# The second pass of a batch set as one block behind chunk 1 of the next first pass, and gathered MoE rows used ten stages after their issue

## The chip, the cores and the metric

One core of a Trainium2 chip runs the whole program. The metric is the device time of one execution in microseconds; the median of three runs of the kernel before is 342.16 us (341.62 to 342.59).

## What is computed

Four batches of q, k and v, each 6208 x 256 in float32. Per batch a cross-covariance attention over the 256 channels, and then a mixture-of-depths MoE over its output: the 128 rows with the highest gate score get a small feed-forward added, all other rows pass through.

```python
qn = q / (np.linalg.norm(q, axis=1, keepdims=True) + 1e-06)   # norm over the 6208 rows
kn = k / (np.linalg.norm(k, axis=1, keepdims=True) + 1e-06)
s = kn.transpose(0, 2, 1) @ qn / tau                          # 256 x 256 a batch
a = softmax(s)                                                # over the last axis
x = v @ a
scores = x @ w_gate
top = the 128 rows of a batch with the highest score
out = x;  out[top] += sigmoid(scores[top]) * (relu(x[top] @ w1) @ w2)
```

## The kernel before

A batch is cut into six chunks of 1024 rows (each partition holds 8 rows of it) and a remainder of 64 rows, counted as chunk 6. Loads convert float32 to bf16 on the way.

**First pass** (`p1_steps`, L195): per row set of 128 rows six matmuls, into the 256 x 256 product of k and q (L210) and into the Gram blocks of q and k (L212, L214), from whose diagonal the norms come. All q and k of a batch have to be in before its softmax. **Softmax** (`softmax_stages`, L222): a generator with three stages; VectorE makes the norms (L229 to L256), a matmul with ones spreads them (L259), then exponentials on ScalarE and the matrix a, with its product with the gate weights, `aw_sb` (L284). **Second pass** (`p2_transpose` L299, `p2_out` L327): per group of four row sets eight transposes of v on TensorE, a copy to SBUF on VectorE (L309), then output matmuls (L343) and score matmuls (L322); ScalarE evicts the output (L348), and a chunk of 1 MB goes out on SyncE's queue (L353). **MoE** (`moe_stages`, L357): a generator that yields between its stages. Stage 1 takes the maximum of the scores, stages 2 to 8 are seven steps of a search for the threshold (VectorE compares and counts, L389, L393, and one small matmul sums over the partitions, L401), stages 9 to 11 make the list of the 128 row numbers `idx` (L427, L438, L453). Then an indirect DMA on POOL's queue gathers these rows of v (`vg`, L455), four yields later TensorE transposes them (L462), multiplies by a (L468), transposes again (L477), does the feed-forward (L495, L503), and a second indirect DMA scatters the updated rows over the output (L510), when the plain stores of that batch have been issued.

**Order.** `phase(b)` (L92) writes out by hand how the chunks of the first pass of batch b and the second pass of batch b-1 follow each other. The list rules two things: the loads (`units`) and, cut into halves of a chunk, TensorE's work (`atoms`). For batches 1 to 3 it is qk0 qk1 v0 v1 qk2 v2 v3 qk3 v4 v5 qk4 v6 qk5 qk6, where qk is of batch b and v of batch b-1. After every atom `slot()` (L526) advances the waiting softmax and the oldest waiting MoE by one stage each. Every engine runs its instructions in the order in which they are written, so a stage that waits on TensorE holds all matmuls behind it, and a gather or scatter that waits on POOL holds all loads behind it.

**Buffers.** q and k have five chunk buffers each, v has six, the outputs nine, the transposed v fourteen. `pump` (L132) issues loads in the order of `units` on POOL's queue as soon as, in the order of the program, the next chunk has a free buffer; it stops at the first that has none.

**The end.** For batch 3 the loop over v makes transposes and scores alone (L579 to L589, with a `slot()` of its own at L589 beside the one after each atom, so two stages a group). Chunks 2 to 6 of the output of batch 2 are held back until then (`deferred`). Then, group by group, one stage of the MoE of batch 3 and the output of one group of batch 3 alternate (L606 to L611), and the rest of that MoE follows.

Of the kernel before, what the change touches and what calls it, by code (L numbers as in the profile page):

```python
# [26 lines left out]
def kernel(  # L27
# [14 lines left out]
    B, N, C = q.shape  # L42
# [7 lines left out]
    NFULL = N // CHUNK  # L50
# [6 lines left out]
    V_BUFS = 6  # L57
    ST_BUFS = 9
    VT_BUFS = 14
    HOLD_FROM = 2  # L60

    const = ctx.enter_context(tc.tile_pool(name="const", bufs=1))
# [2 lines left out]
    rem_pool = ctx.enter_context(tc.tile_pool(name="rem_pool", bufs=2))  # L65
    vt_pool = ctx.enter_context(tc.tile_pool(name="vt_pool", bufs=VT_BUFS))
    st_pool = ctx.enter_context(tc.tile_pool(name="st_pool", bufs=ST_BUFS))
# [24 lines left out]
    def phase(b):  # L92
        if b == 0:
            return [("qk", 0, ci) for ci in range(NFULL + 1)]
        if b == B:
            return [("v", B - 1, ci) for ci in range(NFULL + 1)]
        items = []
        nv = 0
        for ci in range(NFULL + 1):
            items.append(("qk", b, ci))  # L100
            if ci >= 1:
                for _ in range(2 if ci < NFULL // 2 + 1 else NFULL + 1):
                    if nv <= NFULL:
                        items.append(("v", b - 1, nv))
                        nv += 1
        return items

    units = [u for b in range(B + 1) for u in phase(b)]
    loaded = {}
    load_inst = {}  # L110
# [21 lines left out]
    def pump(most=1000):  # L132
        while state["next"] < len(units) and most > 0:
            u = units[state["next"]]
            bk = bucket(u[0], u[2])
            if state[bk] >= limit[bk]:
                return
            emit_load(u)
            state[bk] += 1
            state["next"] += 1  # L140
            most -= 1

    def consumed(u):
        state[bucket(u[0], u[2])] -= 1
        pump()
# [49 lines left out]
    def p1_steps(b, ci):  # L195

        if b not in acc:
            acc[b] = (ps_s.tile([P, 2, C], F32, name="s_ps"), ps_g.tile([P, 4, P], F32, name="g_ps"))
        s_ps, g_ps = acc[b]
        qt, kt = loaded[("qk", b, ci)]  # L200
        rows = RPP if ci < NFULL else 1
        parts = P if ci < NFULL else REM

        def step(s):
            first = ci == 0 and s == 0
            last = ci == NFULL
            qs, ks = qt[:parts, s, :], kt[:parts, s, :]
            for cc in range(2):
                sl = slice(cc * P, (cc + 1) * P)
                nc.tensor.matmul(s_ps[:, cc, :], lhsT=ks[:, sl], rhs=qs,  # L210
                                 start=first and cc == 0, stop=last and cc == 1)
                nc.tensor.matmul(g_ps[:, cc, :], lhsT=qs[:, sl], rhs=qs[:, sl],  # L212
                                 start=first and cc == 0, stop=False)
                nc.tensor.matmul(g_ps[:, 2 + cc, :], lhsT=ks[:, sl], rhs=ks[:, sl],  # L214
                                 start=False, stop=last and cc == 1)

        return [lambda s=s: step(s) for s in range(rows)]
# [94 lines left out]
    def p2_score(b, g, vt_sb, js):  # L312
        ci, s0, n = g
        parts = P if ci < NFULL else REM
        aw_sb = a_tiles[b][1]
        if ci == 0 and s0 == 0 and js[0] == 0:
            sc_tiles[b] = ps_sc.tile([P, NCOL, 2], F32, name="sc_ps")
        sc_ps = sc_tiles[b]
        for j in js:
            col = ci * RPP + s0 + j  # L320
            for cc in range(2):
                nc.tensor.matmul(sc_ps[:parts, col, :], lhsT=vt_sb[:, cc, j, :parts],  # L322
                                 rhs=aw_sb[:, cc, :],
                                 start=cc == 0 and col in (0, NCOL - 1),
                                 stop=cc == 1 and col >= NCOL - 2)

    def p2_out(b, g, vt_sb, scores):  # L327
        ci, s0, n = g
        parts = P if ci < NFULL else REM
        a_sb = a_tiles[b][0]  # L330
        if s0 == 0:
            if ci < NFULL:
                stage_of[(b, ci)] = st_pool.tile([P, RPP, C], F32, name="stage")
            else:
                stage_of[(b, ci)] = rem_pool.tile([P, 1, C], F32, name="stage_rem")
        st = stage_of[(b, ci)]
        for pair in range((n + 1) // 2):
            o_ps = ps_o.tile([P, 2, C], F32, name="o_ps")
            m = min(2, n - pair * 2)
            for pj in range(m):  # L340
                j = pair * 2 + pj
                for cc in range(2):
                    nc.tensor.matmul(o_ps[:parts, pj, :], lhsT=vt_sb[:, cc, j, :parts],  # L343
                                     rhs=a_sb[:, cc, :], start=pj == 0 and cc == 0,
                                     stop=pj == m - 1 and cc == 1)
                if scores:
                    p2_score(b, g, vt_sb, [j])
            nc.scalar.copy(st[:parts, s0 + pair * 2:s0 + pair * 2 + m, :], o_ps[:parts, :m, :])  # L348

    def emit_store(b, ci):  # L350
        st = stage_of.pop((b, ci))
        if ci < NFULL:
            return nc.sync.dma_start(out=view(out, b, ci), in_=st)  # L353
        return nc.sync.dma_start(out=view(out, b, ci), in_=st[:REM, 0, :])


    def moe_stages(b):  # L357
# [29 lines left out]
        for i in range(NSTEP):  # L387
# [18 lines left out]
            if i + 1 < NSTEP:  # L406
# [44 lines left out]
                                op1=ALU.min)  # L451
        idx = moe.tile([P, 1], I32, name="idx", bufs=2)
        nc.vector.tensor_scalar(out=idx, in0=fl, scalar1=float(b * N), scalar2=None, op0=ALU.add)  # L453
        vg = moe.tile([P, C], BF16, name="vg")
        nc.gpsimd.indirect_dma_start(out=vg, out_offset=None, in_=v_flat,  # L455
                                     in_offset=bass.IndirectOffsetOnAxis(ap=idx[:, 0:1], axis=0))
        for _ in range(4):
            yield
        a_sb, _ = a_tiles[b]
        tp = ps_vt.tile([P, 2, 4, P], BF16, name="vt_ps")  # L460
# [41 lines left out]
        for fc in range(NFC):  # L502
# [2 lines left out]
        upd = moe.tile([P, D], F32, name="upd", bufs=2)  # L505
        nc.vector.scalar_tensor_tensor(out=upd, in0=y_ps[:, 0, :], scalar=gate, in1=xe, op0=ALU.mult,
                                       op1=ALU.add)
        while held[b] or (b >= B - 2 and deferred):
            yield
        nc.gpsimd.indirect_dma_start(out=out_flat[0:(b + 1) * N, :],  # L510
# [6 lines left out]
    def advance(lst):  # L517
        while lst:
            try:
                next(lst[0])  # L520
                return True
            except StopIteration:
                lst.pop(0)
        return False

    def slot():  # L526
        advance(smx_side)
        advance(side)
# [31 lines left out]
    def transposes(i, ahead):  # L560

        while tq and tpos[tq[0]] <= i + ahead:
            _, b, g = tq.pop(0)
            vts[(b, g)] = p2_transpose(b, g)
            if g[1] == 4 or g[0] == NFULL:
                consumed(("v", b, g[0]))

    last_groups = []
    for i, a in enumerate(atoms):
        if a[0] == "p1":  # L570
            _, b, ci, lo_, hi_ = a
            pump()
            st = p1_steps(b, ci)
            for f in st[lo_:hi_]:
                f()
            if hi_ != 4:
                consumed(("qk", b, ci))
        elif a[0] == "smx":
            smx_side.append(softmax_stages(a[1]))  # L579
            advance(smx_side)  # L580
        else:
            _, b, g = a
            if b == B - 1:
                transposes(i, 2)
                while b not in a_tiles:
                    advance(smx_side)
                p2_score(b, g, vts[(b, g)], list(range(g[2])))
                last_groups.append(g)
                slot()  # L589
            else:  # L590
                while b not in a_tiles:
                    advance(smx_side)
                p2_out(b, g, vts.pop((b, g)), True)
                if g[1] == 4 or g[0] == NFULL:
                    held[b] -= 1
                    if b == B - 2 and g[0] >= HOLD_FROM:
                        deferred.append((b, g[0]))
                    else:
                        emit_store(b, g[0])
                if g[0] == NFULL:  # L600
                    side.append(moe_stages(b))
        transposes(i, 2)
        slot()
    side.append(moe_stages(B - 1))
    flush_deferred()
    for g in last_groups:  # L606
# [42 lines left out]
```

## Time and profile before

| | us |
|---|---|
| median of three runs | 342.16 (341.62 to 342.59) |
| the profiled execution | 343.5 |
| its span, first to last instruction | 341.4 |
| TensorE matmuls busy | 216.0 (63%) |
| VectorE busy | 139.9 (41%) |
| ScalarE busy | 67.3 (20%) |
| POOL busy | 56.0 (16%) |
| mean granted TensorE clock | 0.807 of 2.4 GHz |

The span is the time between the first and the last instruction that the profiler saw; what lies around it, 2.1 us, belongs to the execution. Busy shares are means over stages with different limits: the first two thirds move nearly all loads, the rest is mostly computation. So the views by stretch and in order of time say more than the table. In them a number in brackets behind an instruction is the time that its engine stood idle before it, and what ended that.

### The profile page before, as it was taken

To read this page: it belongs to the slowest core of one execution; us is meant where nothing else is said; L and a number is where in the kernel's file an instruction comes from. 1 tells how busy PE (TensorE), PEld (TensorE's weight loads), DVE (VectorE), ACT (ScalarE), POOL (GpSimd) and SP (SyncE) were. 2 spreads that over 40 slices of the span, in tenths; PEclk is the share of its full clock that TensorE was granted. 3 is DMA by queue.
4 is the path that set the end of the run, shared out by engine and by line. 5 is a ranking of instruction groups with operands and counts; after the bars stand their busy time and mean duration, and the time that the engine had idled before them with its cause. 6 is when DMAs were issued, how large, how long until landed. Compare 5 with 4: busy or idle time off the path is not lost.

```text
span 341.4 us, 6038 instructions
## 1 busy us (share of the span) xinstructions
PE 216.0 (63%) x2524; PEld 186.0 (54%) x2524; DVE 139.9 (41%) x550; ACT 67.3 (20%) x133; POOL 56.0 (16%) x103
## 2 busy tenths in 40 slices
PE   0878259999575489205898089658981336957350
PEld 0767248999454278204798068647981225835230
DVE  0000044332017796101234889212349895588120
ACT  1000001534200105001450012214500100255410
POOL 7212322110121212030123002101100001100110
PEclk9999767999768599755999569969997555798855
DMA  7999999999999999999879999943594000046800
GB/s 126 213 214 207 213 213 214 213 310 312 323 265 217 213 213 228 316 213 213 294 144 290 245 214 181 293 121 63 99 374 172 0 1 10 17 183 262 307 0 15
DMA packets 17353, 65.90 MB, mean 193 GB/s; under 512 B 1968, under 2 KB 4656, under 8 KB 14256
## 3 DMA queue, kind: packets, MB, share of 16 engines
q0 software_dynamic: 13408, 39.98, 60.5%
q1 hardware_dynamic: 3920, 25.56, 18.6%
q8 instruction: 19, 0.31, 0.3%
q14 instruction: 6, 0.05, 0.0%
HBM read 79.04 MB, written 25.95 MB: 308 GB/s over the span
## 4 chain that ended last, share of the span: by engine, by line
DMA 37%; issue 26%; PE 18%; DVE 11%; POOL 3%; ACT 1%; POOLq 1%; SPq 0%; DVEq 0%; ACTq 0%
DMA k_ch<-in_k_dram 27%; DMA v_ch<-in_v_dram 5%; DMA vg<-in_v_dram,idx 4%; PE o_ps L343 4%; PE s_ps L210 4%; PE vt_ps L306 3%; DVE cnt L393 2%; PE g_ps L214 2%; PE g_ps L212 2%; DVE cmp L389 2%; DMA out_dram<-stage_rem 1%; ACT stage L348 1%; PE o_ps L503 1%; POOL q_ch L124 1%; PE m_ps L259 1%
## 5 line engine op out<-in xcount | busy, mean ns | idle before, releaser
L210 PE MATMUL s_ps<-q_ch,k_ch 128*128 128x256 bf16 x384 | 100.6, 299 | 25.6 <-DMA k_ch<-in_k_dram 25.4
L212 PE MATMUL g_ps<-q_ch 128*128 128x128 bf16 x384 | 90.6, 236 | 0.0
L214 PE MATMUL g_ps<-k_ch 128*128 128x128 bf16 x384 | 90.5, 236 | 0.0
L348 ACT COPY stage<-o_ps 128x512 f32<-128x512 f32 x96 | 53.5, 586 | 109.6 <-PE o_ps L343 109.2
L343 PE MATMUL o_ps<-a_sb,vt_sb 128*128 128x256 bf16 x392 | 60.8, 283 | 1.7 <-ACT stage L348 0.6
L309 DVE COPY vt_sb<-vt_ps 128x1024 bf16<-128x1024 bf16 (+1 forms) x52 | 33.9, 654 | 64.2 <-PE vt_ps L306 63.3
L210 PEld LDWEIGHTS <-k_ch 128*128 128x128 bf16 x384 | 41.1, 107 | 30.9 <-DMA k_ch<-in_k_dram 26.4
L214 PEld LDWEIGHTS <-k_ch 128*128 128x128 bf16 x384 | 41.2, 107 | 8.0
L212 PEld LDWEIGHTS <-q_ch 128*128 128x128 bf16 x384 | 41.1, 107 | 0.3 <-issue 0.3
L322 PEld LDWEIGHTS <-vt_sb 128*128 128x128 bf16 x392 | 34.1, 102 | 9.9 <-issue 4.8
L343 PEld LDWEIGHTS <-vt_sb 128*128 128x128 bf16 x392 | 29.0, 99 | 13.7 <-issue 11.6
L322 PE MATMUL sc_ps<-aw_sb,vt_sb 128*128 128x2 bf16 x392 | 33.2, 167 | 4.8 <-DVE aw_sb L284 4.6
L306 PE MATMUL vt_ps<-ident_b,v_ch 128*128 128x128 bf16 x384 | 33.4, 238 | 0.0
L306 PEld LDWEIGHTS <-v_ch 128*128 128x128 bf16 x384 | 26.1, 107 | 6.2 <-issue 5.9
L124 POOL DMA_DIRECT2D q_ch<-in_q_dram x24 | 13.5, 562 | 59.1 <-PE g_ps L214 30.1
L462 PE MATMUL vt_ps<-ident_b,vg 128*128 128x128 bf16 x8 | 1.6, 300 | 31.8 <-DMA vg<-in_v_dram,idx 31.8
L124 POOL DMA_DIRECT2D v_ch<-in_v_dram x24 | 12.8, 538 | 52.3 <-PE vt_ps L306 15.6
L229 DVE CUSTOM_DVE_ANT_0 junk<-g_ps,ident_f 128x128 f32<-128x128 f32 x16 | 4.6, 290 | 40.3 <-PE g_ps L214 39.9
L259 PE MATMUL m_ps<-diag,ones_f 128*128 128x256 f32 x8 | 4.9, 713 | 24.2 <-DVE diag L256 24.2
L462 PEld LDWEIGHTS <-vg 128*128 128x128 bf16 x8 | 0.5, 110 | 32.5 <-DMA vg<-in_v_dram,idx 32.5
L124 POOL DMA_DIRECT2D k_ch<-in_k_dram x24 | 13.1, 546 | 31.1 <-DMA k_ch<-in_k_dram 11.5
L401 PE MATMUL m_ps<-cnt,ones_b 128*128 128x8 bf16 x28 | 4.7, 168 | 20.8 <-DVE cnt L393 18.9
(118 smaller groups left out, 196.7 us busy)
## 6 DMA issues: line engine op xcount, KB each, us to landing
out_dram<-stage SPq DMA_DIRECT2D x24, 1024.0 KB, 9.8
q_ch<-in_q_dram POOLq DMA_DIRECT2D x24, 512.0 KB, 17.5
k_ch<-in_k_dram POOLq DMA_DIRECT2D x24, 512.0 KB, 18.8
v_ch<-in_v_dram POOLq DMA_DIRECT2D x24, 512.0 KB, 15.1
w_sb<-in_moe_w_dram POOLq DMA_DIRECT2D x2, 512.0 KB, 20.4
out_dram<-stage_rem SPq DMA_DIRECT2D x4, 64.0 KB, 8.0
wg_bcast<-in_moe_w_gate_dram SPq DMA_DIRECT2D x1, 128.0 KB, 3.4
q_rem<-in_q_dram POOLq DMA_DIRECT2D x4, 32.0 KB, 19.1
```

Of the source, the lines that this page charges most:

```text
L124: ins = nc.gpsimd.dma_start(out=t, in_=view(src, b, ci))
L210: nc.tensor.matmul(s_ps[:, cc, :], lhsT=ks[:, sl], rhs=qs, start=first and cc == 0, stop=last and cc == 1)
L212: nc.tensor.matmul(g_ps[:, cc, :], lhsT=qs[:, sl], rhs=qs[:, sl], start=first and cc == 0, stop=False)
L214: nc.tensor.matmul(g_ps[:, 2 + cc, :], lhsT=ks[:, sl], rhs=ks[:, sl], start=False, stop=last and cc == 1)
L259: nc.tensor.matmul(rq_ps[:, 0:C], lhsT=ones_f, rhs=diag.rearrange("p a c -> p (a c)"), start=True, stop=True)
L306: nc.tensor.transpose(vt_ps[:, cc, j, :parts], in_=vt[:parts, s0 + j, cc * P:(cc + 1) * P], identity=ident_b[:parts, :parts])
L309: nc.vector.tensor_copy(vt_sb[:, :, :n, :parts], vt_ps[:, :, :n, :parts])
L322: nc.tensor.matmul(sc_ps[:parts, col, :], lhsT=vt_sb[:, cc, j, :parts], rhs=aw_sb[:, cc, :], start=cc == 0 and col in (0, NCOL - 1), stop= ...
L343: nc.tensor.matmul(o_ps[:parts, pj, :], lhsT=vt_sb[:, cc, j, :parts], rhs=a_sb[:, cc, :], start=pj == 0 and cc == 0, stop=pj == m - 1 and ...
L348: nc.scalar.copy(st[:parts, s0 + pair * 2:s0 + pair * 2 + m, :], o_ps[:parts, :m, :])
L389: nc.vector.tensor_tensor(out=cmp, in0=sc[:, None, :].to_broadcast([P, NTHR, NCOL]), in1=thr[:, :, None].to_broadcast([P, NTHR, NCOL]), op ...
L393: nc.vector.tensor_reduce(out=cnt, in_=cmp, axis=AX.X, op=ALU.add)
```

## The change

`phase` sets the second pass of batch b-1 as one block behind chunk 1 of the first pass of batch b: qk0 qk1 v0 v1 v2 v3 v4 v5 v6 qk2 qk3 qk4 qk5 qk6. Loads and work both follow. In `moe_stages` there is one more yield between the row list and the gather, the number of yields between the issue of the gather and its use goes from four to ten for batches 0 and 1, to five for batch 2 and to two for batch 3, and there is one more yield ahead of the scatter. In the score loop of batch 3 the additional `slot()` goes, so one stage a group is left.

```diff
+    GATHER_WAIT = 10
...
-        items = []
-        nv = 0
-        for ci in range(NFULL + 1):
-            items.append(("qk", b, ci))
-            if ci >= 1:
-                for _ in range(2 if ci < NFULL // 2 + 1 else NFULL + 1):
-                    if nv <= NFULL:
-                        items.append(("v", b - 1, nv))
-                        nv += 1
-        return items
+        qk = [("qk", b, ci) for ci in range(NFULL + 1)]
+        return qk[:2] + [("v", b - 1, ci) for ci in range(NFULL + 1)] + qk[2:]
...
         nc.vector.tensor_scalar(out=idx, in0=fl, scalar1=float(b * N), scalar2=None, op0=ALU.add)
+        yield
         vg = moe.tile([P, C], BF16, name="vg")
         nc.gpsimd.indirect_dma_start(out=vg, out_offset=None, in_=v_flat,
                                      in_offset=bass.IndirectOffsetOnAxis(ap=idx[:, 0:1], axis=0))
-        for _ in range(4):
+
+        for _ in range(GATHER_WAIT if b < B - 2 else (5 if b < B - 1 else 2)):
             yield
...
         nc.vector.scalar_tensor_tensor(out=upd, in0=y_ps[:, 0, :], scalar=gate, in1=xe, op0=ALU.mult,
                                        op1=ALU.add)
+        yield
         while held[b] or (b >= B - 2 and deferred):
             yield
...
                 p2_score(b, g, vts[(b, g)], list(range(g[2])))
                 last_groups.append(g)
-                slot()
```

Counted from the code: the MoE of batch 0 or 1 starts behind the last group of its second pass, with eight halves of the first pass still to come (before: two). Its row list is made in the slot of the softmax, its gather is issued in the slot of the first half of the next batch (on POOL behind the loads up to chunk 4 of that batch for batch 0, up to chunk 4 of batch 3 for batch 1), and the gathered rows are transposed behind group 7 of the next second pass (before: behind the first half of chunk 2 with its transposes, some 4 atoms after the issue). The first eleven stages of the MoE of batch 2 lie beside the halves of chunks 2 to 5 of batch 3, its softmax and the transposes ahead of the first score group; its gathered rows are used behind score group 6.

## Rows read from the trace of the kernel before

**Rows 1.** The page, share of the 16 DMA engines in 40 slices.
```profile
DMA  7999999999999999999879999943594000046800
```

**Rows 2.** POOL in order of time: start, length, instruction, idle time before it.
```profile
81.67 0.56 POOL L124 DMA_DIRECT2D q_ch<-in_q_dram  x1 [4.74 <-PE g_ps L212]
...
91.61 0.53 POOL L124 DMA_DIRECT2D q_ch<-in_q_dram  x1 [4.44 <-DMA k_ch<-in_k_dram]
...
106.26 0.53 POOL L124 DMA_DIRECT2D v_ch<-in_v_dram  x1 [2.08 <-DMA k_ch<-in_k_dram]
...
121.20 0.53 POOL L124 DMA_DIRECT2D k_ch<-in_k_dram  x1 [1.91 <-PE m_ps L401]
...
146.63 1.02 POOL L455 DMA_INDIRECT vg<-in_v_dram,idx  x1 [4.58 <-DMA k_ch<-in_k_dram]
...
169.21 1.00 POOL L510 DMA_INDIRECT out_dram<-upd,idx  x1 [16.36 <-DVE upd L506]
```

**Rows 3.** TensorE in order of time, starts that waited: start, length, instruction, idle time.
```profile
51.83 1.22 PE L259 MATMUL m_ps<-diag,ones_f 128*128 128x256 f32 x2 [4.70 <-DVE diag L256]
...
157.18 0.39 PE L462 MATMUL vt_ps<-ident_b,vg 128*128 128x128 bf16 x2 [18.08 <-DMA vg<-in_v_dram,idx]
...
195.88 1.22 PE L259 MATMUL m_ps<-diag,ones_f 128*128 128x256 f32 x2 [6.49 <-DVE diag L256]
...
225.82 0.39 PE L462 MATMUL vt_ps<-ident_b,vg 128*128 128x128 bf16 x2 [6.36 <-DMA vg<-in_v_dram,idx]
...
264.82 1.22 PE L259 MATMUL m_ps<-diag,ones_f 128*128 128x256 f32 x2 [6.47 <-DVE diag L256]
...
272.21 0.35 PE L322 MATMUL sc_ps<-aw_sb,vt_sb 128*128 128x2 bf16 x8 [4.62 <-DVE aw_sb L284]
...
281.67 0.23 PE L438 MATMUL m_ps<-rhs,oh 128*128 128x51 bf16 x1 [1.55 <-DVE oh L434]
...
298.54 0.49 PE L372 MATMUL m_ps<-dmx,ones_f 128*128 128x128 f32 x2
```

**Rows 4.** Stretches: length, PE, PEld, DVE, ACT, POOL busy, PEclk, DMA share, GB/s.
```profile
60.00:90.00 30.00, 27.22 (x404) 25.27 (x401) 8.30 (x12) 13.48 (x24) 4.28 (x8) 1.00 1.05 286
...
236.80:256.50 19.70, 18.73 (x259) 17.08 (x257) 7.35 (x24) 4.90 (x10) 2.62 (x4) 1.00 0.72 214
256.50:272.20 15.70, 3.42 (x28) 2.39 (x28) 13.83 (x58) 1.45 (x5) 0.00 (x0) 0.63 0.20 82
272.20:286.30 14.10, 5.51 (x78) 5.02 (x77) 10.68 (x44) 0.00 (x0) 1.00 (x1) 0.50 0.04 5
```

**Rows 5.** Landing after issue: gathers at 146.63 and 283.50, load at 172.63.
```profile
DMA to landing us min/median/max: 10.5/10.5/10.5
...
DMA to landing us min/median/max: 2.8/2.8/2.8
...
DMA to landing us min/median/max: 5.2/5.2/5.2
```

**Rows 6.** TensorE in order of time, starts of stages; columns as in rows 3.
```profile
128.71 0.38 PE L343 MATMUL o_ps<-a_sb,vt_sb 128*128 128x256 bf16 x2
...
168.24 0.27 PE L210 MATMUL s_ps<-q_ch,k_ch 128*128 128x256 bf16 x1
...
182.42 0.28 PE L210 MATMUL s_ps<-q_ch,k_ch 128*128 128x256 bf16 x1
...
187.77 0.22 PE L214 MATMUL g_ps<-k_rem 64*128 64x128 bf16 x1
...
209.08 0.38 PE L343 MATMUL o_ps<-a_sb,vt_sb 128*128 128x256 bf16 x2
...
210.62 0.38 PE L343 MATMUL o_ps<-a_sb,vt_sb 128*128 128x256 bf16 x2
...
236.78 0.27 PE L210 MATMUL s_ps<-q_ch,k_ch 128*128 128x256 bf16 x1
```

**Rows 7.** The page, group: count, busy us, mean ns, idle before it.
```profile
L348 ACT COPY stage<-o_ps 128x512 f32<-128x512 f32 x96 | 53.5, 586 | 109.6 <-PE o_ps L343 109.2
```

## The prediction

> **What bounds the kernel now.** Read first the page's slices: the DMA digit is 7 to 9 without a break in the first 26 of 40 slices (some 222 us) and 0 in slices 32 to 35 (some 265 to 299 us) [rows 1]. So the transfers bound the front and something else bounds the rest. Next, what POOL issued in order of time. Loads queued alone are issued 14.94 us apart over six steps, 2.5 us each; while stores run beside them it is 9.94 us over two steps, 5.0 us each [rows 2]. A load and a store of one chunk thus cost 2.5 us each and share the engines, so the time at which something lands while the queue is full is a sum of chunks ahead of it. The same view shows POOL standing still 16.4 us in front of the scatter of batch 0, with no load issued in that time [rows 2].
>
> Then TensorE's starts with their waits [rows 3]. The gather of batch 0 is waited for 18.1 us, that of batch 1 6.4 us, the norms of the softmax 6.5 us in batches 2 and 3 (4.7 in batch 0, where no MoE runs yet). After 157 us no load is waited for at any of these places; what ends each stretch is a gather, or VectorE's chain of softmax and threshold search. So behind 157 us the path is the order of TensorE's instructions, and each stage can be costed by the same stage of before. The last part, from the first matmul of the MoE of batch 3 (298.54) to the end (341.4), is 42.9 us of search, output, gather and feed-forward.
>
> The stage before that is the worst: from 256.5 to 272.2 TensorE is busy 3.4 of 15.7 us, from 272.2 to 286.3 5.5 of 14.1, with DMA at 0.04 and VectorE at 10.7 [rows 4]. There the search of batch 2 stands between softmax 3 and the scores of batch 3.
>
> **The change, part by part.** I call 24 matmuls of the first pass a half (half a chunk), four rows of the second pass a group. Removed: no arithmetic; the 13 extra slots in the score loop of batch 3. Moved: groups of batch b-1 stand together behind chunk 1 of batch b, so a MoE starts 8 halves ahead of the end of its first pass instead of 2, and its first eleven stages lie beside halves of the first pass and beside the softmax. The gather of batches 0 and 1 is issued at the first half of the next batch and used after group 7 of its second pass. POOL's queue changes with the loads: all v loads of a batch stand ahead of chunks 2 to 5, and the gather of batch 0 comes behind the loads of chunk 4 of batch 2. The scatter of batch 0 stays ahead of further loads.
>
> Step 1, the anchor: landing of gather 0. The queue is full from the start in both orders, so work ahead decides. Before it landed at 146.6 + 10.5 = 157.1 [rows 2, 5]. After, chunk 5 of batch 2 and chunk 0 of batch 3 (4 loads, 10.0 us) stand behind it, and one more store (chunk 2 of batch 1) gets in front, +2.5: 149.6. TensorE comes there early: the second pass of batch 1 starts no later than the 128.7 of before [rows 6], its search no longer standing between, and seven groups at 1.54 us (209.08 to 210.62, [rows 6]) take 10.8, so 139.5 at the latest. ACT's two evictions of a group, 0.586 us each [rows 7], stay hidden under 1.54 though no half stands between. A wait of 10 to 14 us remains; ten stages do not cover it. All three stores are issued by then.
>
> Step 2, gather 0 to the next half. Before 157.18 to 168.24, 11.1 us with four groups [rows 3, 6]. After there are five and the remainder: + 1.54 + 0.6 (an estimate, a remainder with its transposes). 149.6 + 13.2 = 162.8.
>
> Step 3, eight halves, the remainder and the search of batch 1. Before, two halves and the remainder beside the first two search steps took 182.42 to 187.99, 5.6 us [rows 6]. Each further half: the stretch 236.8 to 256.5 has six halves, four groups (6.2 us) and two remainders (1.1): (19.7 - 7.3) / 6 = 2.07 [rows 4]. 5.6 + 6 x 2.07 = 18.0, so 180.8. POOL's next load needs the second of these halves, 162.8 + 5.2 = 168.0; the queue has 4 loads and 3 stores (17.5 us) from 149.6 on and is dry for about 1 us.
>
> Step 4, softmax 2 to the second pass. The norms alone 4.7 us, plus one search stage ahead of them, 1.55 (the wait for the one-hot rows) [rows 3]: 187.0. From there before took 195.88 to 209.08, 13.2 [rows 3, 6]; 0.5 of it, an estimate, was search. 199.7 (before 209.08: 9.4 gained).
>
> Step 5, gather 1. Reached at 199.7 + 10.8 = 210.5. Its landing: the load issued at 168.0 into an empty queue lands after 5.2 [rows 5], 13 more at 2.5 make 205.7, and part of two stores (issued about 203 and 206) adds 2.7: 208.4, and with 0.3 to 1.6 us for the gather itself, estimated from the queue's order, under 210. No wait, with a cover of a microsecond: each microsecond by which the loads come later costs one.
>
> Step 6, to the next half: before 225.82 to 236.78, 11.0 [rows 3, 6], plus 2.1 as in step 2, less about 1 because TensorE has not stood idle (bounds 11.1 to 13.1; 12 taken). 222.5. Chunks 2 to 5 of batch 3 and the v loads stand by then: eight loads and a store remain after 208, 22 us, and are wanted between 222 and 255.
>
> Step 7, eight halves with the search of batch 2: 18.0, so 240.5 (before 256.5).
>
> Step 8, softmax 3: before 15.7 [rows 4]. To the norms it took 8.3 (256.5 to 264.82, [rows 3, 4]) with a search step and two copies of transposes in it; after it is between 4.7 + 1.55 = 6.25 and that, 7.6 taken since the copies stay. Then 7.4 as before (264.82 to 272.21, [rows 3]; one search step goes, the index stage comes): 15.0. 255.5.
>
> Step 9, scores of batch 3: before 272.21 to 298.54, 26.3 [rows 3], of which 14.1 - 5.5 = 8.6 idle [rows 4], the search of batch 2 and its gather. The search is done by then, and that gather has six groups of over 1 us each to land in 2.8 [rows 5]. The feed-forward of batch 2 stays. 17.7, so 273.2.
>
> Step 10, the end: same order on TensorE and VectorE, 42.9 us. Fewer waits of batch 3 (2 for 4, plus one ahead) move nothing, since POOL has nothing else queued and the transposes stand behind all output groups in both orders. The deferred stores land before it, as before.
>
> Sum: 298.5 - 273.2 = 25.3 us gained. The span goes from 341.4 to 316.1; the profiled execution took 343.5, 2.1 more than its span and 1.3 over the median. From the median, 342.16 - 25.3 = 316.9.
>
> **Where a page speaks otherwise.** Two places are weighed. The queue is full (DMA 9) while halves and groups alternate [rows 1], and the forecast gives up that alternation. The Trainium skill, "Perfetto Trace Analysis", Optimization Strategy, says that a kernel with several regimes may gain by interleaving them; by that rule setting the second pass whole should cost. What that would be here is the rival "late loads", 325 instead of 316.9. The other is the landing of a gather: 10.5 us with loads queued, 2.8 with none [rows 5]. The Trainium skill, "DMA: Bandwidth & Descriptors", Anatomy of one DMA, gives about 2 us plus bytes over 436 GB/s for one DMA, which has no queue in it. By that rule the gather would not be waited for, the rival "no queue", 302.9; the 10.5 speaks against it here.
>
> **Rivals.** Late loads: the first-pass buffers are full during a whole second pass, so the loads stop until its end, and gather 1 and all behind it come later. For it: step 5 has next to no cover, POOL stood 16.4 us before a scatter [rows 2]. Against: 17.5 us of transfers are queued over that time. With the restart 8 us later (three chunks more ahead, or steps 2 and 3 longer) the time is 325.
>
> No queue: gather 0 lands 2.8 us after its issue, before TensorE gets there, and nothing waits. Then step 3 is bound by the loads of chunk 5: in step 1's sum the v loads of batch 1 are in at 149.6 - 15.0 - 7.5 = 127.1; 8 loads and 6 stores behind them are 35 us, 162.1, plus the last two halves and the remainder, 4.7: 166.8 instead of 180.8. 302.9. Against: the gathers in a full queue took 10.5 [rows 5].
>
> Half clock, the slower one: the long blocks of one kind let TensorE's clock fall. Steps 2 to 7 hold 72 us of TensorE work (13.2 + 18.0 + 10.8 + 12 + 18.0). At 1.2 instead of 2.4 GHz it would double; half of it so is +36, 353, and from 25.3 / 72 = 35% on the gain is gone. Against: the granted clock is 1.00 where TensorE is busy 27.2 of 30 us, halves and groups alike, and falls to 0.50 to 0.63 only where it is busy 3.4 of 15.7 and 5.5 of 14.1 [rows 4].
>
> That the change does not do what it says: the ten stages do not hide gather 0 (step 1), which the forecast has in it.
>
> **How the numbers follow.** Forecast 0.70 (308 to 322: steps 6 and 3 are open by 2 each, step 9 by 3, the anchor by 3), late loads 0.15, no queue 0.06, half clock 0.05, nothing gained 0.04 (a mixture of late loads and half clock). The range 305 to 329 takes in the forecast and most of late loads and leaves out some 0.17. About 0.3%, 1 us, is what a measurement of this kernel can tell from no change (341.62 to 342.59). Faster 0.91 (the first three), within 0.03, slower 0.06.
>
> **What would show it.** TensorE waits for gather 0 some 10 to 14 us until about 150, and for gather 1 hardly. The first matmul of MoE 3 stands near 273, 43 us before the end. Between softmax 3 and it lie no waits for counts. If gather 1 is waited for by over 3 us, late loads; if gather 0 lands by 131, no queue; if the clock in the eight halves around 165 to 180 or 222 to 240 is under 0.9, half clock. The prediction is wrong if a load is waited for after 160 us.

## The result and the profile after

The changed kernel takes 308.94 us (307.58 to 311.6, four runs) where the kernel before, on the same chip, takes 342.38 us: a ratio of 0.9033, interval 0.8965 to 0.91. 33.4 us are gained where 25.3 were forecast; 308.94 lies inside the range 305 to 329, below the forecast's own 316.9. A second measurement gave 308.84 us, ratio 0.9011 (0.8979 to 0.9044). The profiled execution took 307.58 us with a span of 305.5. The forecast for its span was 316.1; of the 10.6 us between them 1.3 and 1.4 come from which executions were profiled (that of before lies above its median, that of after below its own), the rest is terms that were sized too large.

Line numbers of the changed kernel are lower by 7 from the softmax on and by 6 to 4 from the gather on. The page of the changed kernel, 40 slices of 7.6 us: the granted clock and the share of the DMA engines.

```profile
PEclk9999957899998778995589995899999758979865
...
DMA  7999999999999999999996999999999400156700
```

The full stretch [rows 1] now takes the first 31 slices, 237 us, with one 6 at 160 to 168 us, behind the scatter of batch 0. The thin stretch behind it has shrunk from some ten slices to four. The same bytes are moved, and less time stands behind them. POOL in order of time (start, length, instruction, idle time before it and what ended it), changed kernel:

```profile
126.42 1.03 POOL L449 DMA_INDIRECT vg<-in_v_dram,idx  x1 [2.26 <-DVE vt_sb L302]
...
161.81 1.01 POOL L506 DMA_INDIRECT out_dram<-upd,idx  x1 [15.43 <-DVE sc L354]
166.79 0.56 POOL L117 DMA_DIRECT2D q_ch<-in_q_dram  x1 [3.96 <-PE g_ps L207]
...
190.83 1.12 POOL L449 DMA_INDIRECT vg<-in_v_dram,idx  x1 [2.15 <-DVE a_sb L271]
```

Gather 0 is issued 20.2 us earlier than in [rows 2]. POOL still stands 15.4 us in front of the scatter, and the loads resume at 166.79. The scatter is not what holds them: the next load waits 4.0 us more, for the matmuls that free its buffer (L207), as it did before, 2.4 us, at 172.63. TensorE in order of time, the starts by which the steps were forecast (compare [rows 3, 6]):

```profile
149.06 0.39 PE L457 MATMUL vt_ps<-ident_b,vg 128*128 128x128 bf16 x2 [14.29 <-DMA vg<-in_v_dram,idx]
...
162.56 0.28 PE L203 MATMUL s_ps<-q_ch,k_ch 128*128 128x256 bf16 x1
...
186.09 1.22 PE L252 MATMUL m_ps<-diag,ones_f 128*128 128x256 f32 x2 [5.61 <-DVE diag L249]
...
198.10 0.38 PE L336 MATMUL o_ps<-a_sb,vt_sb 128*128 128x256 bf16 x2
...
208.74 0.28 PE L457 MATMUL vt_ps<-ident_b,vg 128*128 128x128 bf16 x2
...
219.56 0.28 PE L203 MATMUL s_ps<-q_ch,k_ch 128*128 128x256 bf16 x1
...
243.54 1.22 PE L252 MATMUL m_ps<-diag,ones_f 128*128 128x256 f32 x2 [5.60 <-DVE diag L249]
...
250.52 0.35 PE L315 MATMUL sc_ps<-aw_sb,vt_sb 128*128 128x2 bf16 x8 [4.18 <-DVE aw_sb L277]
...
263.81 0.49 PE L365 MATMUL m_ps<-dmx,ones_f 128*128 128x128 f32 x2
```

The wait for gather 0 is 14.29 us (18.08 before), that for gather 1 is gone in this execution (6.36 before), and the first matmul of the MoE of batch 3 stands at 263.81 instead of 298.54. Stretches of the changed kernel (columns as in [rows 4]): the eight halves of batches 2 and 3, the softmax of batch 3, the scores of batch 3, the end.

```profile
164.50:179.80 15.30, 14.43 (x183) 12.74 (x183) 13.77 (x53) 0.03 (x1) 5.90 (x11) 1.00 0.94 205
221.50:236.80 15.30, 14.44 (x185) 12.74 (x185) 13.72 (x54) 0.03 (x1) 0.00 (x0) 1.00 1.04 307
236.80:250.50 13.70, 3.42 (x28) 2.42 (x29) 11.63 (x57) 1.46 (x5) 1.01 (x1) 0.63 0.31 114
250.50:263.80 13.30, 12.07 (x210) 10.95 (x209) 9.11 (x24) 1.66 (x4) 0.98 (x1) 0.87 0.01 2
263.80:305.50 41.70, 19.10 (x132) 12.79 (x131) 18.84 (x79) 14.52 (x28) 1.94 (x2) 0.79 0.40 160
```

VectorE's search (13.8 of 15.3 us busy) now lies beside the halves (TensorE 14.4 busy). What TensorE still waits for, whole span of the changed kernel (total us, times, longest):

```profile
PE s_ps L203 <- DMA k_ch<-in_k_dram: 26.2, 6, 9.6
PE m_ps L252 <- DVE diag L249: 21.5, 4, 5.6
PE vt_ps L457 <- DMA vg<-in_v_dram,idx: 18.8, 2, 14.3
```

All six waits for loads lie ahead of 160 us; the two waits for gathered rows are gather 0 and, 4.5 us near the end, the gather of batch 3.

### The profile page after: what moved, and what is told of

Its sections match the earlier page's. It is cut to its first block, busy times and chain, and to the rows that moved or that the text cites. A ratio compares the mean times of both kernels' runs of the same rounds, so it can differ in the third digit from the quotient of the medians.

```text
span 305.5 us, 6039 instructions
## 1 busy us (share of the span) xinstructions
PE 208.8 (68%) x2524; PEld 180.9 (59%) x2524; DVE 141.0 (46%) x550; ACT 67.0 (22%) x133; POOL 56.1 (18%) x103
## 4 chain that ended last, share of the span: by engine, by line
DMA 40%; PE 33%; DVE 17%; issue 5%; ACT 1%; POOLq 0%; POOL 0%; SPq 0%; DVEq 0%; ACTq 0%
DMA k_ch<-in_k_dram 25%; PE s_ps L203 8%; DMA vg<-in_v_dram,idx 7%; PE o_ps L336 6%; DMA v_ch<-in_v_dram 6%; PE vt_ps L299 5%; PE g_ps L205 4%; PE g_ps L207 4%; DVE vt_sb L302 2%; DVE cnt L386 2%; DVE cmp L382 2%; DMA out_dram<-stage_rem 2%; PE m_ps L394 1%; PE m_ps L252 1%; PE sc_ps L315 1%
## 5 line engine op out<-in xcount | busy, mean ns | idle before, releaser
L203 PE MATMUL s_ps<-q_ch,k_ch 128*128 128x256 bf16 x384 | 98.3, 296 | 26.2 <-DMA k_ch<-in_k_dram 26.2
L205 PE MATMUL g_ps<-q_ch 128*128 128x128 bf16 x384 | 89.6, 233 | 0.0
L207 PE MATMUL g_ps<-k_ch 128*128 128x128 bf16 x384 | 89.3, 233 | 0.0
L203 PEld LDWEIGHTS <-k_ch 128*128 128x128 bf16 x384 | 40.5, 106 | 34.0 <-DMA k_ch<-in_k_dram 27.2
L207 PEld LDWEIGHTS <-k_ch 128*128 128x128 bf16 x384 | 40.7, 106 | 7.5
L315 PEld LDWEIGHTS <-vt_sb 128*128 128x128 bf16 x392 | 33.4, 100 | 8.9 <-issue 4.3
L299 PE MATMUL vt_ps<-ident_b,v_ch 128*128 128x128 bf16 x384 | 31.5, 229 | 0.8 <-DVE vt_sb L302 0.8
L299 PEld LDWEIGHTS <-v_ch 128*128 128x128 bf16 x384 | 24.2, 102 | 2.2 <-issue 2.0
L218 ACT COPY s_sb<-s_ps 128x512 f32<-128x512 f32 x4 | 2.3, 586 | 103.8 <-PE s_ps L203 103.8
L117 POOL DMA_DIRECT2D q_ch<-in_q_dram x24 | 13.4, 558 | 45.8 <-DMA k_ch<-in_k_dram 10.9
L386 DVE TENSOR_REDUCE cnt<-cmp 128x8 bf16<-128x392 bf16 x28 | 15.7, 561 | 1.0
L252 PEld LDWEIGHTS m_ps<-diag,ones_f 128*128 128x128 f32 x8 | 2.0, 312 | 23.2 <-DVE diag L249 23.2
```

Source lines behind the costliest of these rows:

```text
L117: ins = nc.gpsimd.dma_start(out=t, in_=view(src, b, ci))
L203: nc.tensor.matmul(s_ps[:, cc, :], lhsT=ks[:, sl], rhs=qs, start=first and cc == 0, stop=last and cc == 1)
L252: nc.tensor.matmul(rq_ps[:, 0:C], lhsT=ones_f, rhs=diag.rearrange("p a c -> p (a c)"), start=True, stop=True)
L299: nc.tensor.transpose(vt_ps[:, cc, j, :parts], in_=vt[:parts, s0 + j, cc * P:(cc + 1) * P], identity=ident_b[:parts, :parts])
L386: nc.vector.tensor_reduce(out=cnt, in_=cmp, axis=AX.X, op=ALU.add)
```

## The experiments

Theory: three gains that follow each other on TensorE's path, namely shorter waits for the gathers, searches beside the halves, and a score stage without a search; what is left of the wait for gather 0 is the queue in front of it. Rivals: one part alone carries the gain; the landing hangs on something other than the queue; what differs from the forecast is the removed slot or VectorE's chain, and not the clock.

### Each part alone: the order, and the waits

The order alone is the kernel before with the new `phase` (the diff); the waits alone are the changed kernel with the old `phase`.

```diff
-        items = []
...
-        return items
+        qk = [("qk", b, ci) for ci in range(NFULL + 1)]
+        return qk[:2] + [("v", b - 1, ci) for ci in range(NFULL + 1)] + qk[2:]
```

> The kernel before with the new order alone: four stages between issue and use of a gather, two stages a score group. Theory (a gather lands behind what was queued before it, so using it earlier also means fewer stores ahead of it): gather 0 is waited for about 17 us and lands near 141 instead of 149, gather 1 about 5 us; the first half behind the second pass of batch 1 comes about 4 us later than the 162.6 of the changed kernel, that of batch 2 about 10 us later; 318 to 321 us. Rival (the ten stages carry a large part of the gain, since seven groups of 1.5 us each no longer stand ahead of either gather): 21 us lost, about 330. Second rival (the order carries all): 308 to 311.

> All of the change but the order: ten stages between gather and use, one stage a score group, the old alternation of halves and groups. Theory: the wait for gather 0 shrinks by about 6 us, that for gather 1 goes, the scores of batch 3 wait less, but the MoE of batch 2 reaches into the output groups of batch 3 and delays the last search; 325 to 335 us. Rival (the order carries all of it): 340 to 345. Rival (the later use carries most of it): 315 to 322.

Order only: 322.79 us, ratio 0.9401 (0.9352 to 0.9449), some 2 us above what was expected; both waits came out longer than expected too (18.27 for 17, 7.43 for 5). Waits only: 323.78 us, ratio 0.9443 (0.9399 to 0.9487), between the two expectations. TensorE in order of time, order only first, then waits only:

```profile
140.99 0.39 PE L454 MATMUL vt_ps<-ident_b,vg 128*128 128x128 bf16 x2 [18.27 <-DMA vg<-in_v_dram,idx]
...
207.98 0.39 PE L454 MATMUL vt_ps<-ident_b,vg 128*128 128x128 bf16 x2 [7.43 <-DMA vg<-in_v_dram,idx]
...
278.41 0.49 PE L364 MATMUL m_ps<-dmx,ones_f 128*128 128x128 f32 x2
```

```profile
162.29 0.39 PE L465 MATMUL vt_ps<-ident_b,vg 128*128 128x128 bf16 x2 [12.50 <-DMA vg<-in_v_dram,idx]
...
255.74 0.35 PE L323 MATMUL sc_ps<-aw_sb,vt_sb 128*128 128x2 bf16 x8 [4.62 <-DVE aw_sb L285]
...
281.09 0.39 PE L373 MATMUL m_ps<-dmx,ones_f 128*128 128x128 f32 x2
```

By TensorE's starts, as in [rows 3]:

| | norms 3 | scores 3 | MoE 3 | span |
|---|---|---|---|---|
| before | 264.82 | 272.21 | 298.54 | 341.4 |
| order only | 255.27 | 262.26 | 278.41 | 321.3 |
| waits only | 248.34 | 255.74 | 281.09 | 320.4 |
| both | 243.54 | 250.52 | 263.81 | 305.5 |

The score stage of both, order only and then waits only (columns as in [rows 4]):

```profile
262.26:278.41 16.15, 14.78 (x210) 12.80 (x210) 9.28 (x24) 1.79 (x4) 1.01 (x1) 0.67 0.03 10
```

```profile
255.74:281.09 25.35, 19.71 (x240) 17.00 (x240) 16.73 (x64) 5.25 (x10) 1.99 (x2) 0.67 0.11 38
```

Each part gains about 20 us, in different places. The waits gain 16.5 us ahead of the scores and 1.0 in the score stage (25.35 for 26.33 us): the search of batch 2 is still in it. They also gain 3.5 us behind it (39.3 for 42.9), as output groups of batch 3 have moved into the score stage (240 matmuls for 217). The order gains 10.0 ahead of the scores and 10.2 in the stage (16.15). Together it is 21.7 and 13.0. Ahead of the scores the parts overlap (16.5 + 10.0 = 26.5 against 21.7). In the stage both together are 2.9 us faster than the order alone with the same 210 matmuls; the mean granted clock is 0.87 there and 0.67 here, so this difference is not shown to come from the waits. "One part alone carries it" fell.

### What sets the landing of gather 0

The order-only run shows what the landing hangs on: its gather 0 is issued at 126.49 with the same loads ahead of it as in the changed kernel (126.42), and landed at 140.94, not 149.02, as its expectation had it (near 141). DMA transfers issued between 126 us and the landing, order only and then changed kernel (KB each, us to landing):

```profile
k_ch<-in_k_dram POOLq DMA_DIRECT2D x2, 512.0 KB, 14.9
...
vg<-in_v_dram,idx POOLq DMA_INDIRECT x1, 14.5
```

```profile
out_dram<-stage SPq DMA_DIRECT2D x3, 1024.0 KB, 11.8
...
vg<-in_v_dram,idx POOLq DMA_INDIRECT x1, 22.6
```

The changed kernel has three stores in that time, the order-only kernel has none: its TensorE stops four stages behind the issue, at 122.7, before the first store's chunk is done. The ten stages that are to cover the gather produce the stores that delay it. TensorE gets 12.1 us further (134.8 for 122.7) and the gather comes 8.1 us later, so the wait shrinks by 4.0 only. Three changes of the queue put this to the test. The first sets gather 0 behind the next loads:

```diff
+        if b == 0:
+            yield
         vg = moe.tile([P, C], BF16, name="vg")
...
-        for _ in range(GATHER_WAIT if b < B - 2 else (5 if b < B - 1 else 2)):
+        for _ in range(GATHER_WAIT - (b == 0) if b < B - 2 else (5 if b < B - 1 else 2)):
```

> The changed kernel with gather 0 issued one stage later, so that it stands behind the loads of the next chunk too; its use stays where it is. Theory (gather 0 lands when the loads ahead of it have landed, and TensorE waits for it at a fixed place of its program, so the end moves by what the landing moves): it lands with the next chunk's loads, about 5 us later than the 149.02 of the changed kernel, the wait grows from 14.3 to 19 or 20 us, and the time is 312.5 to 316 us. Rival (the landing is set by something other than its place in the queue, such as the stores beside it): the landing stays within 2 us and the time is 307 to 311 us.

314.53 us, ratio 0.9161 (0.9133 to 0.9188). It landed at 154.30, 5.3 us later where about 5 was expected, though it was issued 10.2 us later:

```profile
154.35 0.39 PE L459 MATMUL vt_ps<-ident_b,vg 128*128 128x128 bf16 x2 [19.96 <-DMA vg<-in_v_dram,idx]
```

The second sets both gathers ahead of loads, by holding the loads of batch b + 2 from chunk 4 on until the gather of batch b is issued; the third from chunk 3 on.

```diff
+            if u[0] == "qk" and u[1] >= 2 and u[2] == 4 and u[1] - 2 not in gathered:
+                return
...
+        gathered.add(b)
+        pump()
```

> The changed kernel, the gathers of batches 0 and 1 issued on POOL ahead of the loads of chunk 4 instead of behind them; nothing else moved. Theory (the landing is the sum of chunks ahead): gather 0 lands with chunk 3, near 141 instead of 149.0, TensorE waits 6 us instead of 14.3, all behind it comes 8 us earlier; 299.5 to 303 us. Rival (a gather lands by its own time and the wait has another cause): 307 to 311.

> As the run before it, the gathers ahead of the loads of chunk 3. Theory: gather 0 lands near 131, before TensorE gets there at 134.6, so that wait goes; then the loads of chunk 5 of batch 2 (near 160) are the next bound, close to where TensorE comes; 292 to 298 us. Rival (the loads become the bound earlier, since POOL waits for the row numbers ahead of three chunks): 300 to 309.

Ahead of chunk 4: 304.33 us, ratio 0.8878 (0.8824 to 0.8931), short of the expectation, as the gather landed at 144.20 and not at 141: the place of two loads is worth 4.8 us here, much as the 5.3 in the run before, and not the 8 that I had put down. Ahead of chunk 3: 298.51 us, ratio 0.8695 (0.866 to 0.873), half a microsecond above its expectation; the gather landed at 135.0 and not near 131, so a little of the wait is left. The two waits for gather 0, and a load that is now late in the third kernel:

```profile
144.24 0.39 PE L462 MATMUL vt_ps<-ident_b,vg 128*128 128x128 bf16 x2 [10.96 <-DMA vg<-in_v_dram,idx]
```

```profile
135.04 0.29 PE L462 MATMUL vt_ps<-ident_b,vg 128*128 128x128 bf16 x2 [1.79 <-DMA vg<-in_v_dram,idx]
...
162.20 0.28 PE L207 MATMUL s_ps<-q_ch,k_ch 128*128 128x256 bf16 x1 [1.95 <-DMA k_ch<-in_k_dram]
```

Then the stores themselves, with the gather left where the change has it:

```diff
+        if b == 1 and ci < 3:
+            return nc.sync.dma_start(out=view(out, b, ci)[:, 0:1, :], in_=st[:, 0:1, :])
```

> The changed kernel with the first three stores of batch 1 (issued at 127 to 133 us, beside the loads ahead of gather 0) cut to one of their eight rows per partition; the other rows of these chunks are not stored. Theory (gather 0 lands when the transfers ahead of it are done, stores beside it included: in the changed kernel the loads land 5 us apart while these stores run and 2.5 us apart otherwise): four loads at 2.5 us from 130.65 on and a little for the gather and the small stores, so a landing at 141.5 to 142.5 instead of 149.02, a wait of 6.5 to 8 us instead of 14.29, and the time falls by about as much, to 300.5 to 303.5 us. Rival (the landing is set by the loads ahead alone, or by the gather's own time of 22 us from its issue): the landing stays at 147 to 149 us and the time at 307 to 311 us.

302.1 us, ratio 0.8797 (0.8769 to 0.8826), inside the theory's range. Transfers issued from 126 us to the landing, and the wait:

```profile
out_dram<-stage SPq DMA_DIRECT2D x3, 128.0 KB, 7.9
...
vg<-in_v_dram,idx POOLq DMA_INDIRECT x1, 16.8
```

```profile
143.09 0.39 PE L459 MATMUL vt_ps<-ident_b,vg 128*128 128x128 bf16 x2 [6.43 <-DMA vg<-in_v_dram,idx]
```

The landing is at 143.04, 6.0 us earlier and half a microsecond later than expected. The wait is 6.43 us; 1.9 of the 7.9 by which it shrank come from TensorE, which got there at 136.7 in this execution instead of 134.8. Landing against median: 154.30 and 314.5, 149.02 and 308.9, 144.20 and 304.3, 143.04 and 302.1. Over these 11.3 us of landing the end moves by 12.4, about one for one; from there to 135.0 and 298.5 it moves by 3.6 for 8, since the wait is used up but for 1.79 us. So the wait that the change left is shown to be the queue, stores beside it as well as loads ahead: 2.4 to 2.6 us of landing for each load moved (4.8 and 5.3 for two), and 2.3 for each MB not stored (6.0 for 2.6). The Trainium skill, "DMA: Bandwidth & Descriptors", Queues, rings and completion order, says that each engine takes turns between the queues that have work for it, a packet at a time; the issue times agree: loads go out 2.5 us apart without stores and 5.0 beside them [rows 2].

### The score stage and the clock

The step furthest off was the score stage, 13.3 us instead of 17.7. In the changed kernel the granted clock rises from 0.50 to 1.00 at 254.0, 3.5 us into it; before, it stood at 0.50 until 294.8. First the same kernel again:

> The changed kernel unaltered, once more, to see how far the time from the first scores of batch 3 to the first matmul of its MoE repeats: 13.3 us in the profile of the changed kernel, where the granted clock rose to 1.00 after 3.5 us; 16.3 us in two other runs where it stayed at 0.50 for most of the stage. If that is the clock alone, this run shows a value between 13 and 16.5 us that goes with the time of the rise, and 307 to 311 us; if 13.3 us belongs to the kernel, it shows 13.3 us whatever the clock does.

308.84 us. The stage took 13.68 us, with the rise 4.6 us into it. The same stretch in five kernels, first scores to first matmul of MoE 3: this one, the one with small stores, the two with the gather ahead of chunk 3 and behind chunk 5, and the one with added matmuls that is told next (columns as in [rows 4]).

```profile
250.31:263.99 13.68, 12.47 (x210) 11.34 (x210) 9.13 (x24) 1.68 (x4) 0.98 (x1) 0.83 0.01 2
```

```profile
244.04:258.08 14.04, 12.90 (x210) 11.74 (x209) 9.14 (x24) 1.67 (x4) 0.98 (x1) 0.79 0.01 2
```

```profile
238.72:255.06 16.34, 15.56 (x211) 14.33 (x210) 9.31 (x24) 1.79 (x4) 0.98 (x1) 0.59 0.01 2
```

```profile
254.95:271.27 16.32, 15.55 (x210) 14.32 (x209) 9.32 (x24) 1.78 (x4) 0.98 (x1) 0.59 0.01 2
```

```profile
255.08:267.20 12.12, 10.88 (x210) 9.71 (x209) 9.04 (x24) 1.67 (x4) 0.98 (x1) 1.00 0.00 1
```

The instructions are the same, the clock differs (0.83, 0.79, 0.59, 0.59, 1.00) and the time follows it: 12.12 at full clock throughout, and about 0.33 us more for each microsecond at half clock (rises after 3.5, 4.6, 5.8 and 13.4 us: 13.3, 13.7, 14.0, 16.3). "13.3 us whatever the clock does" fell. The last of the five has matmuls whose result nobody reads, placed where TensorE stands idle: ahead of the norms matmul (batches 2 and 3), of the scores and of the transposes of `vg` (batch 3).

```diff
+    def filler(n):
+        w = ps_o.tile([P, 2, C], F32, name="o_ps")
+        for _ in range(n):
+            nc.tensor.matmul(w[:, 0, :], lhsT=ones_b, rhs=w1_sb[:, 0, 0:C], start=True, stop=True)
...
+        if b >= 2:
+            filler(40)
...
+        if b == 3:
+            filler(32)
...
+        if b == 3:
+            filler(20)
```

> The changed kernel with matmuls added whose result nobody reads: 40 while TensorE waits for the softmax norms of batches 2 and 3, 32 ahead of the scores of batch 3, 20 ahead of the transposes of the gathered rows of batch 3. Theory (the rest of step 9's gain and of steps 4, 8 and 10 hangs on the clock granted after TensorE's idle stretches: 0.5 at 182.3 to 192.5, 240.3 to 254.0 and 271.1 to 274.5 in the changed kernel): the norms matmuls take about half, the scores stage takes 11 to 12 us in place of 13.3, and the time is 300 to 304 us. Rival (VectorE's chain bounds these stretches, or the added matmuls hold up what is queued behind them): 308 to 312 us.

309.61 us, ratio 0.9 (0.8962 to 0.9039): no gain, as the rival said, but not for its reason. The stage took 12.1 us, as the theory wanted. The gain was lost in the middle, at gather 1:

```profile
211.47 0.39 PE L468 MATMUL vt_ps<-ident_b,vg 128*128 128x128 bf16 x2 [5.05 <-DMA vg<-in_v_dram,idx]
```

In the changed kernel TensorE used it at 208.74 without a wait. SyncE's stores of that stretch, changed kernel and then this one (start, length, instruction):

```profile
201.45 30.51 SPq L346 DMA_DIRECT2D out_dram<-stage  x6
```

```profile
198.96 33.28 SPq L355 DMA_DIRECT2D out_dram<-stage  x6
```

A faster TensorE issues the first store of batch 2 2.5 us earlier, beside the last loads ahead of gather 1, and the k load in front of the gather lands at 208.78 instead of 205.35. The second execution of the changed kernel lies between the two: first store at 199.72, and a short wait.

```profile
208.49 0.29 PE L457 MATMUL vt_ps<-ident_b,vg 128*128 128x128 bf16 x2 [1.32 <-DMA vg<-in_v_dram,idx]
```

That these stores are the cause was not tested by itself here; for gather 0 it was. Next, the same matmuls were added where gathers come earlier, ahead of chunk 3:

> The kernel that issues each gather ahead of the loads of chunk 3 of the next first pass, with the same added matmuls as in the filler run. It differs from the run without them (298.5 us) in the clock alone, where the scores stage took 16.3 us at a granted clock of 0.5 for most of it. Theory (the clock after idle stretches has a price of 4 to 8 us here): 289 to 294 us, scores stage 11 to 13 us. Rival (the added matmuls stand on the path, or the clock falls anyway): 298 to 301 us.

296.3 us, ratio 0.8616 (0.8583 to 0.865), between the two expectations and 2 to 3 us under the kernel without them; its score stage took 12.1 us. The loads of chunk 5 are now waited for 3.6 us, and gather 1 is late there too:

```profile
197.73 0.29 PE L473 MATMUL vt_ps<-ident_b,vg 128*128 128x128 bf16 x2 [3.66 <-DMA vg<-in_v_dram,idx]
```

One chunk further ahead for this gather:

```diff
-            if u[0] == "qk" and u[1] >= 2 and u[2] == 3 and u[1] - 2 not in gathered:
+            if u[0] == "qk" and u[1] >= 2 and u[2] == (3 if u[1] == 2 else 2) and u[1] - 2 not in gathered:
```

> The kernel with the gathers ahead of the loads of chunk 3 and the added matmuls, with the gather of batch 1 one chunk further ahead, in front of the loads of chunk 2 of batch 3. There TensorE waited 3.7 us for this gather, which landed at 197.7. Theory (a place in the queue moved by two loads moves the landing by two transfers): landing about 192.5, no wait, 292 to 294.5 us. Rival (the loads of chunk 2 come later by the same amount and are waited for in its place): 296 to 297 us.

292.88 us, ratio 0.8537 (0.8514 to 0.8561), the best of all, some 16 us under the changed kernel. Gather 1 landed at 187.89, earlier than the 192.5 expected, most likely because the first store beside it goes out at 185.53 only; it is not waited for:

```profile
192.81 0.28 PE L473 MATMUL vt_ps<-ident_b,vg 128*128 128x128 bf16 x2
```

But the added matmuls don't hold the clock in this run: the gather of batch 2, used in the score stage, is now late, and behind that wait the clock is at 0.50 from 241.9 to 245.4. The stage took 14.85 us instead of 12.1.

```profile
239.93 0.29 PE L473 MATMUL vt_ps<-ident_b,vg 128*128 128x128 bf16 x2 [2.04 <-DMA vg<-in_v_dram,idx]
```

```profile
234.13:248.98 14.85, 12.15 (x210) 10.96 (x209) 9.19 (x24) 1.78 (x4) 0.98 (x1) 0.89 0.28 99
```

### The slot in the score loop

```diff
                 last_groups.append(g)
+                slot()
```

> The changed kernel with the call of slot() after each scores tile put back, so that up to two stages are emitted per group while scores run. Theory (what the score loop emits beside the scores is beside the path, since no item is due there that another stage waits for): the same as the changed kernel within 1.5 us, 307 to 311 us. Rival (the removed call is part of the gain of step 9, where the scores stage took 13.3 us in place of the 17.7 forecast; stages put between scores of one group delay the next ones by 3 to 5 us): 312 to 316 us.

310.84 us, ratio 0.9075 (0.9046 to 0.9103): inside the theory's range, but 2 us above both measurements of the changed kernel (0.9033 and 0.9011; the first interval overlaps this one, the second ends just below it). Its score stage:

```profile
250.06:266.14 16.08, 14.44 (x210) 12.52 (x209) 9.18 (x24) 1.78 (x4) 0.98 (x1) 0.69 0.03 10
```

The clock rose only 9.9 us into it. By the rate above that alone makes 15.4 of the 16.1 us. The order-only run, which has the slot too, shows much the same stage (16.15 us at 0.67). Whether the denser stages between the scores put the rise off, or it fell so by chance, these profiles don't tell, as the rise came later still (13.4 us) in two runs without the slot. That stays open; the slot is worth 0 to 2 us.

## Why the prediction was right, and where its sizes were off

By the forecast's own steps, as forecast and as measured (us; the last column is what each step took beyond its forecast, and adds up to the 10.6 us between the spans):

| step | forecast | after | off in this step |
|---|---|---|---|
| 1 gather 0 used | 149.6 | 149.06 | -0.5 |
| 2 next half | 162.8 | 162.56 | +0.3 |
| 3 halves and search 1 done | 180.8 | 179.79 | -0.8 |
| 4 second pass of batch 2 | 199.7 | 198.10 | -0.6 |
| 5 gather 1 used | 210.5 | 208.74 | -0.2 |
| 6 next half | 222.5 | 219.56 | -1.2 |
| 7 halves and search 2 done | 240.5 | 236.79 | -0.8 |
| 8 scores of batch 3 | 255.5 | 250.52 | -1.3 |
| 9 MoE of batch 3 | 273.2 | 263.81 | -4.4 |
| 10 end of span | 316.1 | 305.5 | -1.2 |

- **Right: the anchor.** Counting what lies ahead of gather 0 gave 149.6; it landed at 149.02. TensorE came at 134.8 and waited 14.29 us, at the upper end of "10 to 14". Step 1 has all three stores in its sum, one more than before, at 2.5 us each; three were worth 8.1 us by the order-only run, and a store of 1 MB 2.3 us by the run with small stores. What it did not say is that the ten stages of cover themselves bring these stores, so that most of what the cover gives is taken back.
- **Right: the path.** In both profiles of the changed kernel no load is waited for after 160 us, the searches are beside the halves, and gather 1 has hardly any cover: no wait in one profile of the changed kernel, 1.32 us in the other, 5.05 when TensorE runs 2.5 us ahead.
- **Off: step 9, "17.7".** I took the busy time of before at the clock of before. The term has two errors. With the clock at half for 13.4 us the stage takes 16.3, so 1.4 was too much at any clock: TensorE was busy 16.70 us before, with 217 matmuls, and 15.56 with 211 in the run at 16.34; I put the difference down to the search of batch 2, whose matmuls I had not taken out. The other 3.0 is the clock: before it stayed at half to 294.8, with TensorE busy 5.5 of the first 14.1 us [rows 4]; now it rises 3.5 us into the stage. A busy stage is not enough for that, since in the run at 16.34 TensorE was busy 15.56 and the clock still stayed at half for 13.4 us. The forecast held this step open by 3 us, and it was off by 4.4. The stretch of before, same columns as [rows 4]:

```profile
272.21:298.54 26.33, 16.70 (x217) 14.38 (x216) 17.32 (x64) 1.79 (x4) 2.01 (x2) 0.57 0.04 9
```

- **Off by about a microsecond each, all to the same side:** steps 3 and 7 (a half with its search step is 1.94 us, not 2.07), step 6 (10.8 for 12, under the lower bound of 11.1, at a clock of 1.00 where it was 0.81 before), step 8 (norms 6.75 us behind the halves for 7.6, scores 7.0 behind them for 7.4) and step 10 (41.7 for 42.9, at a clock of 0.79 where it was 0.73). Durations read from stretches that held waits of their own carried some of these waits into the sum, and so did a lower clock; for steps 6, 8 and 10 that is argued, not tested.
- **Luck.** 308.94 lies just above the lower end of the forecast's own 308 to 322, with nine of ten steps off to the same side. Where in the score stage the clock rose was no part of the forecast; had it risen as late as in the run at 16.34, the time would have been some 3 us longer (an estimate from the stage's 13.3 and 16.3 us).
- **Rivals.** "Late loads" fell for the changed kernel, though a late gather 1 came true in the run with added matmuls, there behind earlier stores and not behind full buffers, as far as the traces show. The Trainium skill, "Perfetto Trace Analysis", Optimization Strategy, says that interleaving regimes may help; order only, which gives the alternation up, gained 20 us, and the measurement decides here. "No queue" fell: 22.6 us to landing. "Half clock" fell: 1.00 in both stretches of halves.

## What to carry to other kernels

In this kernel a transfer issued early into a full queue is not early: count the loads ahead of it and the stores that its cover will issue meanwhile, and move its place in the queue rather than its use. Ten stages of cover bought 4 us on one wait, while moving both gathers two chunks ahead in the queue bought 10 us of the whole time. When a stage loses its waits, don't cost it with the durations of before: look at which level the clock stood there and give the stage at both levels. And after each engine that gets faster, look for the transfer that is now the late one.

## What the hardware showed that I had not expected

The same 210 matmuls of the score stage took 12.1 us at a granted clock of 1.00 and 16.3 us at a mean of 0.59, and which of these a run gets hangs on when, within the stage, the clock rises: 3.5 to 13.4 us into it, without a change in the stage itself. It was 3.5 and 4.6 us in two executions of the changed kernel; what sets it was not tested. And a gather issued at the same time behind the same loads took 14.5, 16.8 or 22.6 us to land, by the bytes stored beside it: none, three of 128 KB, three of 1 MB.
